# Carrying phases from chunk to chunk: an addition in place instead of a transfer or a matrix product, and three kinds of edges in TensorE's order

## The chip, the core and the metric

One core of one Trainium2 chip. The time is the device time of one launch in microseconds (us). Three runs of the kernel before gave a median of 533.52 us, from 533.45 to 533.83.

## What is computed

A gated linear attention, then a mixture of experts that picks one expert per token. Batch 4, 8 heads, 768 tokens, head size 48; 3072 rows of 384 for the experts, 8 experts with 1024 hidden units, all float32.

```python
mag = np.sqrt(a_re * a_re + a_im * a_im)
scale = np.minimum(mag, 0.999) / (mag + 1e-06)
a_re_n, a_im_n = (a_re * scale, a_im * scale)
for t in range(S):
    ar, ai = (a_re_n[:, :, t, :, None], a_im_n[:, :, t, :, None])
    new_re = ar * S_re - ai * S_im
    new_im = ar * S_im + ai * S_re
    kv = np.einsum('bhd,bhe->bhde', k[:, :, t], v[:, :, t])
    S_re, S_im = (new_re + kv, new_im)
    y[:, :, t] = np.einsum('bhd,bhde->bhe', q[:, :, t], S_re)
# x: y as 3072 rows of 384
e_idx = np.argmax(x @ w_gate, axis=1)
# out = softmax gate * sigmoid gate * relu(x @ w1[e]) @ w2[e], e = e_idx of the row
```

## The kernel before, in words

The complex decay of a step is written as a length and an angle. The lengths of a batch up to a token are then running sums of logarithms, and the angles are running sums too, so a chunk of 128 tokens can be computed at once: q and k are scaled by the running length and turned by the running angle, and what is left are ordinary products of matrices, with a state of 96 x 48 per head that passes from chunk to chunk.

There are 24 chunks of 128 tokens (6 per batch, 4 batches), a token to a partition and the 384 numbers of 8 heads along it. Chunks are prepared in groups of 1, 1, 2, 2, and then 3 chunks. For a group, `prep_exp` makes the logarithms of the lengths and the tangents of the angles on ScalarE and VectorE; `decay` takes the running sum of the logarithms with a matrix product by a triangle (L521, tile `cs`), exponentials of it, and scales q and k; `prep_trig` takes the arctangent; `turns` takes the running sum of the angles (L574, also `cs`), in units of whole turns; `phase` takes the sine and the cosine (tile `trig`). ScalarE holds one set of function tables at a time, so it changes between exponentials and sines with a load (L228).

The sum of the angles goes over a batch, not a chunk, so each chunk needs the last row of the chunk before. After the sum, VectorE rounds it (L578), subtracts the whole turns (L579, in place of the angles, tile `ai`) and takes the size for the cosine (L585). The last row, on partition 127, is the carry. There are two ways for it. Up to the fourth group (`g <= CARRY`), 32 rows of the result are multiplied by a matrix that has ones for the last of them (L576, `sel`), into the same bank as the sum of the next chunk. From the fifth group on, the row is moved to partition 0 by a transfer on SyncE's queue (L584, 18 times), and VectorE adds it to the first row of the next chunk's angles before their sum is taken (L556, 15 times; the first chunk of a batch takes none).

Per chunk, the main order is: turn k (L622, 8 transposes at L94, copy L632), half of the scores (L664, mask L665), turn q, the other half, the gates' rows of the chunk before (`rows_and_gates`, L245; L705 copies the rows to `xn`, which is stored), `state` (L644 brings in the old state, L649 adds the new products, L653 scales it) and `values` (L678 products of the scores with v, L684 of q with the state, both into `xo`; L688 copies it). Sums, phases and the routing are mixed into that order, some chunks ahead.

In the attention stage the order on each engine isn't written by hand. A scheduler takes the instructions as the program gives them, with a rank (`urge` moves some ahead) and its own estimate of when inputs are there. `after(ins, prev, ...)` adds an edge for the order of one engine alone, with no wait on a semaphore. The experts' stage (L1172, L1235) starts near 280 us and is not touched; nor is the recurrence as a fallback, in a branch that these inputs don't take, except that it gets a new copy of its inputs.

## Time and profile before

| | |
|---|---|
| median of 3 runs | 533.52 us (533.45 to 533.83) |
| the profiled execution | 535.06 us, span 533.3 us |
| busy: TensorE, VectorE, ScalarE | 93%, 64%, 59% of the span |
| granted TensorE clock, mean | 0.97 |

The span is the time from the first to the last instruction of the profiled execution. Engines: PE is TensorE (PEld its loads of weights), DVE VectorE, ACT ScalarE, POOL GpSimd, SP SyncE, and SPq is what SyncE issues to the DMA engines. L574 is line 574 of the kernel before. The granted clock is a share of 2.4 GHz.

### The profile page before, as it was taken

The page shows a single profiled execution, that of the slowest core. Times are in us where ns is not written, and L with a number is a line of the kernel's source. Part 1 is how long each engine was busy: PE and PEld are TensorE (multiplying, and loading weights), DVE is VectorE, ACT ScalarE, POOL GpSimd, SP SyncE. Part 2 cuts the span into 40 slices and gives each one's busy share as a digit, 9 for nine tenths or more (in the row PEclk, how much of TensorE's full clock was granted, in tenths as well). Part 3 has the DMA queues.
Part 4 walks back from the last instruction along what each step waited for, and adds up shares of the span by engine and source line. Part 5 has one row for each costly group of instructions (what it writes and reads, how often), then busy time and mean ns, then how long its engine had stood idle before and what let it go on. Part 6 is the DMA issues. An engine that isn't in the chain of part 4 may idle for free.

```text
span 533.3 us, 10970 instructions
## 1 busy us (share of the span) xinstructions
PE 495.2 (93%) x4191; PEld 427.8 (80%) x4191; DVE 340.6 (64%) x801; ACT 314.2 (59%) x581; POOL 116.3 (22%) x134
## 2 busy tenths in 40 slices
PE   2899896999989999999989899999999999999992
PEld 0378574877877878778787789999999999999992
DVE  5579678998877988898857646444353636355220
ACT  7678677887858789657624236355452726354220
POOL 4002002030110203033310544412334232111112
PEclk9799989999989999999999799999999999999998
DMA  8664542526235321104424565537163544431001
GB/s 285 199 216 137 120 132 61 164 67 179 72 75 149 45 77 49 29 31 135 143 56 145 161 170 180 165 82 235 44 205 120 173 149 142 142 115 50 15 27 45
DMA packets 46898, 63.84 MB, mean 120 GB/s; under 512 B 11769, under 2 KB 38668, under 8 KB 46836
## 3 DMA queue, kind: packets, MB, share of 16 engines
q1 hardware_dynamic: 38708, 53.63, 33.6%
q0 software_dynamic: 8128, 9.42, 6.2%
q8 instruction: 35, 0.57, 0.5%
q14 instruction: 27, 0.22, 0.2%
HBM read 53.92 MB, written 9.88 MB: 120 GB/s over the span
## 4 chain that ended last, share of the span: by engine, by line
PE 59%; issue 16%; DVE 8%; DMA 7%; ACT 5%; POOL 3%; POOLq 0%; SPq 0%; DVEq 0%; ACTq 0%
PE acc L1172 12%; PE up L1235 11%; PE tr L94 6%; PE sc L664 5%; PE cs L574 4%; PE xo L678 4%; PE tr L245 4%; PE cs L521 3%; POOL out_dram L1185 3%; PE xo L684 2%; DMA carry<-ai 2%; PE st L649 2%; DMA xd<-xn 1%; DMA ar<-in_a_re_dram 1%; DMA raw<-in_moe_w_dram 1%
## 5 line engine op out<-in xcount | busy, mean ns | idle before, releaser
L1240 DVE SCALAR_TENSOR_TENSOR hl<-up,hh 128x464 fp32r<-128x464 f32 (+7 forms) x64 | 37.7, 589 | 69.8 <-ACT hh L1239 69.5
L1239 ACT ACTIVATE hh<-up 128x464 fp32r<-128x464 f32 (+7 forms) x64 | 33.0, 516 | 72.5 <-PE up L1235 72.5
L1235 PE MATMUL up<-xh,w1h 128*128 128x464 f32 (+7 forms) x192 | 69.1, 360 | 0.2 <-ACT xh L1022 0.2
L1235 PE MATMUL up<-xl,w1h 128*128 128x464 f32 (+7 forms) x192 | 68.1, 355 | 0.0
L1235 PE MATMUL up<-xh,w1l 128*128 128x464 f32 (+7 forms) x192 | 67.8, 353 | 0.0
L1172 PE MATMUL acc<-hh,w2h 128*128 128x464 f32 (+6 forms) x168 | 61.8, 368 | 0.0
L1172 PE MATMUL acc<-hl,w2h 128*128 128x464 f32 (+6 forms) x168 | 59.8, 359 | 1.5 <-DVE hl L1240 1.5
L1172 PE MATMUL acc<-hh,w2l 128*128 128x464 f32 (+6 forms) x168 | 59.8, 356 | 0.0
L1185 POOL DMA_INDIRECT out_dram<-y,sid x28 | 31.7, 1134 | 125.2 <-ACT y L1207 122.2
L664 PE MATMUL sc<-qt,kt 96*128 96x128 f32 x384 | 52.4, 279 | 0.0
L664 PEld LDWEIGHTS sc<-qt,kt 96*128 96x128 f32 x384 | 47.2, 191 | 3.3 <-issue 1.7
L1116 POOL DMA_INDIRECT rows<-xd,sid x28 | 35.5, 1267 | 57.7 <-DVE w1l L211 29.2
L211 DVE TENSOR_TENSOR w1l<-raw,w1h 128x512 fp32r<-128x512 f32 x48 | 30.7, 685 | 18.9 <-ACT w1h L210 18.8
L678 PE MATMUL xo<-scores,v 128*48 128x128 f32 x384 | 42.7, 279 | 0.0
L211 DVE TENSOR_TENSOR w2l<-raw,w2h 128x512 fp32r<-128x512 f32 x48 | 30.6, 688 | 14.6 <-ACT w2h L210 14.3
L1062 POOL DMA_INDIRECT table<-entry,addr x20 | 28.1, 1404 | 53.5 <-DVE addr L1058 49.3
L1235 PEld LDWEIGHTS up<-xl,w1h 128*128 128x128 f32 x192 | 36.3, 189 | 1.6 <-DVE xl L1023 0.4
L210 ACT CAST w1h<-raw 128x512 fp32r<-128x512 f32 x48 | 27.1, 619 | 17.9 <-DMA raw<-in_moe_w_dram 17.9
L1235 PEld LDWEIGHTS up<-xh,w1h 128*128 128x128 f32 x192 | 36.5, 190 | 1.3 <-ACT xh L1022 0.4
L544 POOL COPY rcs<-rcs 24x48 f32<-24x48 f32 (+2 forms) x10 | 5.4, 540 | 146.2 <-DMA rcs<-re 95.6
L1235 PEld LDWEIGHTS up<-xh,w1l 128*128 128x128 f32 x192 | 36.4, 190 | 1.0
L684 PE MATMUL xo<-qt,state 96*48 96x128 f32 x320 | 36.7, 276 | 0.0
(213 smaller groups left out, 1117.9 us busy)
## 6 DMA issues: line engine op xcount, KB each, us to landing
raw<-in_moe_w_dram SPq DMA_DIRECT2D x32, 768.0 KB
ar<-in_a_re_dram SPq DMA_DIRECT2D x24, 192.0 KB
ai<-in_a_im_dram SPq DMA_DIRECT2D x24, 192.0 KB
k<-in_k_dram SPq DMA_DIRECT2D x24, 192.0 KB
q<-in_q_dram SPq DMA_DIRECT2D x24, 192.0 KB
v<-in_v_dram SPq DMA_DIRECT2D x24, 192.0 KB
xd<-xn SPq DMA_DIRECT2D x24, 192.0 KB
rows<-xd,sid POOLq DMA_INDIRECT x28, 4.3
```

Of the source, the lines that this page charges most:

```text
L94: return nc.tensor.transpose(out=out, in_=in_, identity=ident[p0:p0 + n, p0:p0 + n])
L211: nc.vector.tensor_tensor(out=lo[:, s], in0=raw[:, s], in1=hi[:, s].bitcast(F32), op=ALU.subtract)
L664: nc.tensor.matmul(sp[:, j * P:(j + 1) * P], r["kt"][:D2, h, :], r["qt"][:D2, h, :], start=True, stop=True)
L678: nc.tensor.matmul(op[u * DP:u * DP + D, j * P:(j + 1) * P], vt[c][:, h * D:(h + 1) * D], r["s"][:, h, :], start=True, stop=(cc == 0))
L684: nc.tensor.matmul(op[u * DP:u * DP + D, j * P:(j + 1) * P], xs[:D2, h * D:(h + 1) * D], r["qt"][:D2, h, :], start=False, stop=True)
L1062: ins = nc.gpsimd.indirect_dma_start(out=table, out_offset=bass.IndirectOffsetOnAxis(ap=addr[:, c:c + 1], axis=0), in_=entry[:, c, :], in_ ...
L1116: ins = nc.gpsimd.indirect_dma_start(out=rows[e % 2][:n, i, :], out_offset=None, in_=xd[:known], in_offset=bass.IndirectOffsetOnAxis(ap=id ...
L1172: nc.tensor.matmul(accs[kt][:, :cap], w[:, cs], a, start=(ft == 0 and s == 0), stop=(ft == FT - 1 and s == 2))
L1185: ins = nc.gpsimd.indirect_dma_start(out=out, out_offset=bass.IndirectOffsetOnAxis(ap=id_of(e, i, n, loaded), axis=0), in_=y[:n, :], in_of ...
L1235: nc.tensor.matmul(up[:, :cap], w[:, kt, :], x[:, kt, :], start=(m == 0), stop=(m == 3 * KT - 1))
L1239: nc.scalar.activation(out=hh, in_=up[:, :cap], func=AF.Relu)
L1240: nc.vector.scalar_tensor_tensor(out=hl, in0=up[:, :cap], scalar=0.0, in1=hh.bitcast(F32), op0=ALU.max, op1=ALU.subtract)
```

## The change

The inputs a_re and a_im are reordered on the host: in each chunk, the first token comes last. The triangles of the two running sums are changed to match (`tri_ring`: a strict triangle with a full last row), so that the sums come out in the order of the tokens. The row to which the carry belongs is then on partition 127, as the carry is. VectorE adds it in place, on partitions 96 to 127, with a column that is 2 pi on the last partition and 0 on the others; this is done in all groups. The transfers (L584), the matrix products by `sel` (L576) and two variants that weren't in use go. In TensorE's order, three edges are added: a running sum comes behind the last product of `values` that the program has given so far; the first product of a `state` comes behind the last product of the gates' rows; the first product of `values` comes behind the last one of `state`. The fallback recurrence gets its a_re and a_im in order again by four copies in DRAM, inside its branch.

```diff
+    def tri_ring(name, val):
+        t = tri(name, val, strict=True)
+        nc.gpsimd.affine_select(
+            out=t, in_=t, pattern=[[0, P]], compare_op=ALU.is_ge, fill=val, base=P - 2, channel_multiplier=-1)
+        return t
+    tri_l = tri_ring("tri_l", 0.5)
+    tri_t = tri_ring("tri_t", 1.0 / (2.0 * math.pi))
-    tri_r, tri_o, sel (two casts to F32R, a square mask of ones in the last row)
+    last = const.tile([P, 1], F32, name="last")          # 2 pi on partition 127, else 0
...
+            def behind_values(ins):
+                if "values" in st:
+                    after(ins, st["values"], "values first")
...
@@ decay @@
-                    if g >= SPLIT:
-                        ...
-                    else:
-                        nc.tensor.matmul(lp[:, :HD], tri_l, d["l2"][:, c, :], start=True, stop=True)
+                    ins = nc.tensor.matmul(lp[:, :HD], tri_l, d["l2"][:, c, :], start=True, stop=True)
+                    behind_values(ins)
@@ carried, turns @@
-                if not first and not plain:
-                    nc.vector.scalar_tensor_tensor(
-                        out=fr[0:1, :], in0=st["carry"], scalar=2.0 * math.pi, in1=fr[0:1, :], op0=ALU.mult, op1=ALU.add)
+                if (starts[g] + c) % NC:
+                    row = G[g]["ai"][96:128, c, :]
+                    nc.vector.scalar_tensor_tensor(
+                        out=row, in0=st["carry"], scalar=last[96:128], in1=row, op0=ALU.mult, op1=ALU.add)
...
-                    nc.tensor.matmul(tp[:, :HD], tri_t, fr, start=True, stop=first or not plain)
-                if not first and plain:
-                    nc.tensor.matmul(tp[:, :HD], sel[96:128], st["carry"], start=False, stop=True)
+                ins = nc.tensor.matmul(tp[:, :HD], tri_t, fr, start=True, stop=True)
+                behind_values(ins)
...
-                if g <= CARRY:
-                    st["carry"] = fr[96:128, :]
-                else:
-                    st["carry"] = early.tile([1, HD], F32, name="carry")
-                    nc.sync.dma_start(out=st["carry"], in_=fr[127:128, :])
+                st["carry"] = fr[96:128, :]
@@ state @@
+                    after(ins, sets["gates"], "rows first")          # ins: the product by ident, L644
-                        nc.tensor.matmul(
+                        st["state"] = nc.tensor.matmul(
@@ values @@
+                        if h == 0:
+                            after(ins, st["state"] if cc < NC - 1 else sets["gates"], "states first")
...
+                if cc:
+                    st["values"] = ins
@@ recurrence (fallback) @@
+            a_re_of, a_im_of = in_order("a_re_of", a_re), in_order("a_im_of", a_im)
@@ host @@
+        if name in ("a_re", "a_im"):
+            a = _np.ascontiguousarray(_np.roll(a.reshape(a.shape[0], -1, P, *a.shape[2:]), -1, axis=2).reshape(a.shape))
```

## Rows read from the trace of the kernel before

**Rows 1.** The page: TensorE and the other engines' busy time, share of the span and instructions, and the granted clock in 40 slices of 13.3 us, in tenths.
```profile
PE 495.2 (93%) x4191; PEld 427.8 (80%) x4191; DVE 340.6 (64%) x801; ACT 314.2 (59%) x581; POOL 116.3 (22%) x134
PEclk9799989999989999999999799999999999999998
```

**Rows 2.** Busy time by stretch: from and to, length, busy time (instructions) of TensorE, its weight loads, VectorE, ScalarE, GpSimd, then the granted clock, the DMA engines' share and GB/s.
```profile
127.00:159.00 32.00, 30.04 (x335) 24.40 (x332) 26.92 (x63) 23.92 (x41) 4.26 (x4) 0.96 0.37 100
...
189.00:236.00 47.00, 46.99 (x512) 37.24 (x511) 41.25 (x114) 38.61 (x71) 8.35 (x7) 1.00 0.16 44
```

**Rows 3.** Instructions in order of time (start, duration, engine, line, what): the copy of a chunk's rows on ScalarE, once per chunk. Between the first and the second row lie nine chunks, between the second and the third five.
```profile
99.22 0.48 ACT L705 COPY xn<-tr 128x384 f32<-128x384 f32 x1
...
189.35 0.48 ACT L705 COPY xn<-tr 128x384 f32<-128x384 f32 x1 [0.80 <-PE tr L245]
...
235.77 0.48 ACT L705 COPY xn<-tr 128x384 f32<-128x384 f32 x1
```

**Rows 4.** The chain that ended last, in order of time: start, length of the piece, what. Its three pieces of the carry's transfer.
```profile
87.07 3.34 DMA carry<-ai
...
119.57 4.21 DMA carry<-ai
...
150.07 4.87 DMA carry<-ai
```

**Rows 5.** Groups of instructions by line: busy us, mean ns of one, then the engine's idle time just before them and what ended it. A matrix product of float32 is two records.
```profile
L574 PE MATMUL cs<-ai,tri_t 128*128 128x384 f32 x48 | 23.4, 578 | 12.8 <-DVE ai L556 7.2 <-POOL rcs L544 3.0 <-ACT ai L234 2.6
...
L234 ACT ACTIVATE trig<-ai 128x384 f32<-128x384 f32 x24 | 12.6, 524 | 8.7 <-DVE ai L579 8.4
...
L556 DVE SCALAR_TENSOR_TENSOR ai<-carry,ai 1x384 f32<-1x384 f32 x15 | 8.2, 545 | 5.4 <-DMA carry<-ai 5.4
...
L576 PE MATMUL cs<-ai,sel 32*128 32x384 f32 x10 | 6.0, 690 | 0.1
```

**Rows 6.** Instructions in order of time, 149 to 156 us. In brackets: idle time of the engine before, and what ended it.
```profile
149.25 0.54 DVE L579 TENSOR_TENSOR ai<-cs,rnd 128x384 f32<-128x384 f32 x1
...
151.56 0.95 DVE L622 TENSOR_TENSOR qc<-q,trig 128x768 f32<-128x768 f32 x1
...
152.97 0.64 PE L94 MATMUL tr<-ident,qc 128*96 128x128 f32 x4
...
154.97 0.55 DVE L556 SCALAR_TENSOR_TENSOR ai<-carry,ai 1x384 f32<-1x384 f32 x1 [2.45 <-DMA carry<-ai]
...
155.57 0.93 PE L574 MATMUL cs<-ai,tri_t 128*128 128x384 f32 x2 [1.96 <-DVE ai L556]
```

**Rows 7.** Busy time by stretch, columns as in rows 2: behind two of the waits.
```profile
91.00:95.50 4.50, 4.38 (x14) 2.25 (x14) 4.50 (x7) 3.52 (x7) 0.00 (x0) 0.62 0.70 168
...
156.00:160.00 4.00, 4.00 (x26) 3.57 (x26) 3.20 (x8) 1.48 (x3) 0.00 (x0) 0.57 0.18 49
```

**Rows 8.** Instructions in order of time, 123 to 125 us.
```profile
123.81 0.55 DVE L556 SCALAR_TENSOR_TENSOR ai<-carry,ai 1x384 f32<-1x384 f32 x1 [1.67 <-DMA carry<-ai]
...
124.41 0.91 PE L574 MATMUL cs<-ai,tri_t 128*128 128x384 f32 x2 [0.95 <-DVE ai L556]
```

**Rows 9.** Instructions in order of time, 88 to 95 us.
```profile
88.34 1.25 ACT L234 ACTIVATE t<-lnr,b_eps 128x1152 f32<-128x1152 f32 x1 [3.01 <-DVE lnr L481]
...
90.43 0.55 DVE L556 SCALAR_TENSOR_TENSOR ai<-carry,ai 1x384 f32<-1x384 f32 x1 [0.56 <-DMA carry<-ai]
...
90.91 1.34 DVE L490 SCALAR_TENSOR_TENSOR l<-lnr,t 128x1152 f32<-128x1152 f32 x1
91.12 1.28 PE L574 MATMUL cs<-ai,tri_t 128*128 128x384 f32 x2 [4.27 <-DVE ai L556]
91.34 0.60 ACT L234 ACTIVATE trig<-rnd,b_cos 128x384 f32<-128x384 f32 x1
...
92.78 0.94 DVE L622 TENSOR_TENSOR kc<-k,trig 128x768 f32<-128x768 f32 x1
...
93.77 1.60 PE L94 MATMUL tr<-ident,kc 128*96 128x128 f32 x8
```

**Rows 10.** Instructions in order of time, 16 to 20 us: the first two chunks' phases.
```profile
16.72 0.56 DVE L578 TENSOR_SCALAR rnd<-cs 128x384 f32<-128x384 f32 x1 [2.30 <-PE cs L574]
17.38 0.56 DVE L579 TENSOR_TENSOR ai<-cs,rnd 128x384 f32<-128x384 f32 x1
...
18.09 1.61 PE L576 MATMUL cs<-ai,sel 32*128 32x384 f32 x2
...
19.74 0.56 DVE L578 TENSOR_SCALAR rnd<-cs 128x384 f32<-128x384 f32 x1 [1.41 <-PE cs L576]
```

**Rows 11.** The chain that ended last, in order of time: sums inside a run of products with v, the first and the last of five such places.
```profile
106.89 0.84 PE cs L574 x2
107.73 0.79 PE xo L678 x10
...
237.98 0.84 PE cs L574 x2
238.83 0.36 PE xo L684 x4
```

**Rows 12.** Instructions of VectorE in order of time, 84 us.
```profile
84.00 0.54 DVE L556 SCALAR_TENSOR_TENSOR ai<-carry,ai 1x384 f32<-1x384 f32 x1
84.47 0.15 DVE L1058 TENSOR_SCALAR addr<-row 128x2 uint32<-128x2 f32 x1
```

More of the change, by code (lines that the diff above doesn't have):

```diff
@@ L103, in tri @@
         return t
-    tri_l = tri("tri_l", 0.5)
-    tri_r = const.tile([P, P], F32R, name="tri_r")
-    nc.gpsimd.tensor_copy(out=tri_r, in_=tri_l)
-    tri_t = tri("tri_t", 1.0 / (2.0 * math.pi))
+    def tri_ring(name, val):
[5 more added lines that the diff above has]
+    tri_t = tri_ring("tri_t", 1.0 / (2.0 * math.pi))
     mask = tri("mask", 1.0)
-    tri_o = const.tile([P, P], F32R, name="tri_o")
-    nc.gpsimd.tensor_copy(out=tri_o, in_=mask)
     tri_s = tri("tri_s", 1.0, strict=True, dt=BF16)
@@ L114, in tile_gated_attention_moe @@
     nc.gpsimd.memset(ones_b, 1.0)
-    sel = const.tile([P, P], F32, name="sel")
-    nc.gpsimd.memset(sel, 1.0)
+    last = const.tile([P, 1], F32, name="last")
+    nc.gpsimd.memset(last, 2.0 * math.pi)
     nc.gpsimd.affine_select(
-        out=sel, in_=sel, pattern=[[0, P]], compare_op=ALU.is_ge, fill=0.0,
-        base=-(P - 1), channel_multiplier=1,
-    )
+        out=last, in_=last, pattern=[[0, 1]], compare_op=ALU.is_ge, fill=0.0, base=-(P - 1), channel_multiplier=1)
     iota = const.tile([P, CAP], F32, name="iota")
@@ L550, in carried, with turns @@
             def carried(g, c):
-                first = (starts[g] + c) % NC == 0
-                fr = G[g]["ai"][:, c, :]
-                plain = st["carry"] is not None and st["carry"].shape[0] > 1
-                if not first and not plain:
+                if (starts[g] + c) % NC:
+                    row = G[g]["ai"][96:128, c, :]
                     nc.vector.scalar_tensor_tensor(
-                        out=fr[0:1, :], in0=st["carry"], scalar=2.0 * math.pi, in1=fr[0:1, :], op0=ALU.mult, op1=ALU.add)
-                return first, plain
-            def turns(g, c, taken=None):
-                first, plain = taken or carried(g, c)
+                        out=row, in0=st["carry"], scalar=last[96:128], in1=row, op0=ALU.mult, op1=ALU.add)
+            def turns(g, c, taken=False):
+                if not taken:
+                    carried(g, c)
                 fr = G[g]["ai"][:, c, :]
                 tp = pp.tile([P, 512], F32, name="cs")
-                if g >= TSPLIT:
-                    ah = early.tile([P, HD], F32R, name="ah", bufs=AHB)
-                    al = early.tile([P, HD], F32R, name="al", bufs=AHB)
-                    nc.vector.tensor_scalar(out=ah, in0=fr, scalar1=TURN, scalar2=None, op0=ALU.mult)
-                    nc.vector.scalar_tensor_tensor(
-                        out=al, in0=fr, scalar=TURN, in1=ah.bitcast(F32), op0=ALU.mult, op1=ALU.subtract)
-                    nc.tensor.matmul(tp[:, :HD], tri_o, ah, start=True, stop=False)
-                    nc.tensor.matmul(tp[:, :HD], tri_o, al, start=False, stop=True)
-                else:
-                    nc.tensor.matmul(tp[:, :HD], tri_t, fr, start=True, stop=first or not plain)
-                if not first and plain:
-                    nc.tensor.matmul(tp[:, :HD], sel[96:128], st["carry"], start=False, stop=True)
+                ins = nc.tensor.matmul(tp[:, :HD], tri_t, fr, start=True, stop=True)
+                behind_values(ins)
                 rnd = early.tile([P, HD], F32, name="rnd", bufs=4)
@@ L579, in turns @@
                 nc.vector.tensor_tensor(out=fr, in0=tp[:, :HD], in1=rnd, op=ALU.subtract)
-                if g <= CARRY:
-                    st["carry"] = fr[96:128, :]
-                else:
-                    st["carry"] = early.tile([1, HD], F32, name="carry")
-                    nc.sync.dma_start(out=st["carry"], in_=fr[127:128, :])
+                st["carry"] = fr[96:128, :]
                 nc.vector.tensor_scalar(
@@ L591, in turning @@
                 for c in range(sizes[g]):
-                    taken = carried(g, c)
+                    carried(g, c)
                     yield
-                    turns(g, c, taken)
+                    turns(g, c, True)
                     yield
```

17 lines of the change are left out of this document (11 added, 6 removed).

## The prediction, made before the changed kernel was run

> **What bounds the kernel now.** I read the page's engine table and clock line first [rows 1]: TensorE is busy for 93% of the span, and the granted clock falls under 9 tenths in five of the 40 slices, three of them in the first 160 us. The change touches only the attention stage, which ends near 280 us, so next come the busy time in two stretches of it and the pace of its chunks [rows 2, 3]. From 189 to 236 us TensorE has no idle time to speak of, and five chunks pass between the copies at 189.35 and 235.77: 9.28 us each, which I take for TensorE's own pace. From 99.22 to 189.35 nine chunks take 90.13 us, 10.01 each: 0.73 x 9 = 6.6 us above that pace. So there is time to win before 189 us and next to none behind it; what is won upstream is kept, since TensorE's later work stays the same. The chain that ended last says where it lies: three pieces of it are the transfer that brings a chunk's last row of phases to partition 0, 3.34, 4.21 and 4.87 us [rows 4]. The groups by line say what these cost the engines [rows 5]: VectorE stood 5.4 us before the 15 additions of the carry (L556), and TensorE stood 7.2 us before the running sums of the turns (L574) because of them.
>
> **The change, part by part.** *The carry without a transfer.* 18 transfers and 15 additions on one partition go; 20 additions on partitions 96 to 127 come (chunks 1 to 5 of four batches), with the same 384 elements to a partition, so 0.545 us each by L556 [rows 5]. Without the transfer the addition can stand right behind the subtraction (L579) that makes the carry. Place by place:
>
> A, 149 to 157 us [rows 6]. The carry is there at 149.25 + 0.54 = 149.8; the addition starts at 154.97, the sum at 155.57. TensorE ends the transposes of 152.97 at 153.61 and stands for 1.96 us. What is late next: the other four transposes of the same qc, which was made from 151.56 to 152.51. They could go at once, so the whole wait goes. Behind it the clock was granted at 0.57 from 156 to 160 us [rows 7], between the levels of 1.2 and 2.4 GHz, after TensorE had stood: (1 - 0.57) x 4 = 1.7 us of full-clock work lost. Take 1.96 + 1.7 = 3.7 us; at least 0 (something else late), at most the chain's 4.87 [rows 4].
>
> B, 123 to 125 us [rows 8]. VectorE stands 1.67 us, TensorE 0.95. Take 0.95; 0 to 1.67.
>
> C, 86 to 95 us [rows 9]. TensorE stands 4.27 us before the sum at 91.12, and the clock is 0.62 from 91 to 95.5 us [rows 7], another 0.38 x 4.5 = 1.7 us. But here something else is late next: the transposes at 93.77 need kc, made from 92.78 to 93.72, which needs sines and cosines that end at 91.94, and these stand behind an exponential that ends at 89.59 and a load of function tables. Without the addition and the 0.56 us before it VectorE could start L490 at 89.87 instead of 90.91, and kc at 91.94, some 0.85 us earlier. Take 0.85; 0 to 4.27 + 1.7 = 6.0.
>
> The rest of VectorE's 5.4 us, 5.4 - 2.45 - 1.67 - 0.56 = 0.7, made TensorE wait nowhere (1.96 + 0.95 + 4.27 is its 7.2 already): 0, up to 0.7.
>
> *The early chunks*, where the carry was a second matrix product (L576) into the same bank. Five of these go, 6.0 us of records [rows 5], and an addition takes the place of each; but the old product followed a sum that was already done, and the new sum must wait for the addition. The product at 18.09 lets the rounding start at 19.74, 1.65 us [rows 10]. Now an addition of 0.545 comes first, then a sum of the same columns at the same low clock: 0.55 us later. For the other four the sum is shorter at full clock or TensorE has transposes between: some 0. Take +0.5; from -1 (TensorE freed) to 5 x 0.545 = +2.7.
>
> *Queues and set-up.* SyncE loses 18 issues and their waits; loads and row stores that stand behind them leave earlier, but loads run chunks ahead: 0. The carry is now read by VectorE only, so a tile of phases comes free no later. GpSimd's set-up swaps two casts and a square mask for two selections and a column, hidden behind the first loads and logarithms; uncovered, under 1 us. The host's reordering is before the launch, and the loads keep shapes and sizes. The copies in the fallback recurrence are in a branch that isn't taken: 0.
>
> *TensorE's order.* Three kinds of edges without waits of their own: sums behind the last products with v traced so far, a state's first product behind the gates' rows, the products with v behind the state. The work is unchanged. Sums do lie inside runs of products in the trace: 0.84 us at 106.89, with ten records of products after it, and five such places from there to 237.98 [rows 11]. Moving one back brings the copy of its products some 0.84 us forward and its own phase back by about the run's rest, 0.79 us. Take 0; from -2 (half of 5 x 0.84) to the +8.4 of the last rival.
>
> *VectorE's hand-over.* The addition on one partition overlaps its follower: it starts at 84.00 and lasts 0.54, the follower starts at 84.47, 0.07 us before its end [rows 12]. Where the follower needs the result there is a gap instead: 16.72 + 0.56 = 17.28, next start 17.38, 0.10 us [rows 10]. If an addition at partition 96 loses the overlap on both sides, that is 20 x 2 x (0.07 + 0.10) = 6.8 us of VectorE at worst; half is paid anyway where it directly follows its own input, and VectorE, busy 26.92 of 32 and 41.25 of 47 us [rows 2], has room for most. Take +0.5; 0 to +6.8. The Trainium skill, VectorE: DVE Perf Modes, section Two Vector instructions with no wait between them, has this as a rule: an instruction whose inputs or output start in another group of 32 partitions than the last one's begins only when every earlier one has finished. It speaks against this change; no run here shows it yet.
>
> **Sum.** -3.7 - 0.95 - 0.85 + 0.5 + 0 + 0.5 = -4.5 us. The profiled execution took 535.06 us (the span of 533.3 and 1.8 around it), so it would take 530.6; the median of the runs, 533.52, lies 1.54 lower, which gives **529.0 us**.
>
> **Rivals.** *All of it comes back.* If the scheduler, with no transfer to wait for, also moves what is late next in C, TensorE's 7.2 us and both losses of clock (3.4) go: 533.5 - 10.6 + 0.5 = 523.4. For: the stretch before 189 us runs far above the pace. Against: the table loads fix when sines can be made.
>
> *The wait was hidden.* If in A the next thing is late too (ScalarE's copies, the mask of the scores on VectorE), B and C give 1.8 us, and the early chunks and a hand-over of 1.3 us instead of 0.5 take them back: 533.5. For: VectorE is busy for 0.84 to 0.88 of those stretches. The skill's rule above would make this one likelier. Against: in A VectorE itself stood.
>
> *Sums too late: slower.* TensorE takes its queue in order; a sum behind products can't fill the time while these wait for the mask. ScalarE already stands 8.4 us for turned phases [rows 5]. It decides if the sum's phase is the next thing that ScalarE needs. A run is 32 records, 2.5 us at the 0.79 us for ten [rows 11]; a sum that would have gone inside it loses two thirds, 1.7 us; at five places +8.4, less the 4.5 won: 537.4. Against: most sums feed phases that are used a group later.
>
> **How the numbers follow.** Forecast 0.58 (its own range 525.5 to 532), all of it back 0.14, hidden 0.13, slower 0.15. A measurement of this kernel can tell about 0.2%, 1.07 us, from no change: faster 0.58 + 0.14 = 0.72, same 0.13, slower 0.15. The range reaches from 523.0, just past the first rival, to 535.0, past the hidden wait with 1.5 us of the unknown costs; it leaves out the last rival and a little at the bottom.
>
> **What would show it.** Right: the addition within 1 us of its subtraction; under 2 us of TensorE standing before L574's line for it; no fall of the clock near 150 us; nine chunks between the copies that now lie at 99.22 and 189.35 in 85 to 87 us; the pace behind unchanged at 9.3. Wrong: TensorE standing as long at the same places for sines or masks; gaps around the additions on VectorE of several us in all; ScalarE's wait for turned phases grown beyond 8.4 us; or a gain of this size behind 189 us, where I expect none.

## The result, and the profile after

The changed kernel took **538.43 us** (median of 20 runs, 534.99 to 541.52) beside 533.53 (531.10 to 541.29) for the kernel before on the same chip: ratio 1.0078, 95% interval 1.0055 to 1.0102. It is slower by some 0.8%; I had forecast 529.0. Some executions of either kernel run slower than the rest; each ratio here and below leaves these out, and so isn't the quotient of the two medians. A second set of runs gave 537.29 beside 532.85, ratio 1.0073 (1.0047 to 1.0100). The two profiled executions lie closer together than the medians, 536.20 us (span 534.5) against 535.06, so both kernels were profiled once more: before 531.15, changed 536.45. That pair differs by 5.3 us, like the medians, and stages are compared in it unless another is named.

Of the signs that I had named for being right, three came: the addition stands right behind its subtraction, the clock doesn't fall near 150 us, and the pace behind is about what it was. The nine chunks went faster than I had named. The fifth failed: TensorE stands 8.6 us for the addition before the running sums, where I had named under 2. The page of after, answering to [rows 1]: TensorE is busy for less, VectorE for 8.4 us more, and the clock falls to 5, 8 and 7 tenths in the fourth, sixth and eighth slice.
```profile
PE 486.9 (91%) x4181; PEld 427.2 (80%) x4181; DVE 349.0 (65%) x806; ACT 313.9 (59%) x581; POOL 117.4 (22%) x134
PEclk9995989799999999999998899999999999999998
```
Busy time by stretch in the changed kernel, columns as in [rows 2]; the second row is the place of step A.
```profile
127.00:159.00 32.00, 31.02 (x397) 25.14 (x397) 28.84 (x66) 24.94 (x44) 6.01 (x4) 1.00 0.40 112
149.00:157.00 8.00, 8.00 (x115) 6.37 (x115) 7.10 (x14) 4.79 (x9) 5.61 (x4) 1.00 0.44 94
189.00:236.00 47.00, 46.68 (x572) 37.61 (x571) 43.70 (x114) 37.69 (x69) 8.69 (x8) 1.00 0.15 45
```
TensorE has no idle time at A and the full clock. The addition stands right behind its subtraction, as here on VectorE near 155 us (against the 5.2 us from carry to addition in [rows 6]):
```profile
154.72 0.56 DVE L568 TENSOR_TENSOR ai<-cs,rnd 128x384 f32<-128x384 f32 x1
155.31 0.62 DVE L555 SCALAR_TENSOR_TENSOR ai<-ai,last 32x384 f32<-32x384 f32 x1
155.96 0.36 DVE L570 TENSOR_SCALAR rnd<-ai 128x384 int32<-128x384 int32 x1
```
And the pace: the copies of [rows 3] are now these, the nine chunks take 84.14 us (forecast 85 to 87, before 90.13) and the five behind 9.43 each.
```profile
104.35 0.48 ACT L695 COPY xn<-tr 128x384 f32<-128x384 f32 x1
...
188.49 0.48 ACT L695 COPY xn<-tr 128x384 f32<-128x384 f32 x1 [0.33 <-PE tr L245]
...
235.65 0.48 ACT L695 COPY xn<-tr 128x384 f32<-128x384 f32 x1 [0.48 <-PE tr L245]
```
But the first of them lies 5.1 us later than before. What was won behind 100 us had been lost ahead of it. The groups by line, answering to [rows 5]: TensorE stands longer for the addition (8.6 us) than it did for the carry (7.2), and 14.4 us for the logarithms of the decays (tile `l`), where it was 9.4.
```profile
L564 PE MATMUL cs<-ai,tri_t 128*128 128x384 f32 x48 | 22.9, 561 | 11.6 <-DVE ai L555 8.6 <-POOL rcs L545 3.0
L234 ACT ACTIVATE trig<-ai 128x384 f32<-128x384 f32 x24 | 12.6, 525 | 6.7 <-DVE ai L568 6.6
L555 DVE SCALAR_TENSOR_TENSOR ai<-ai,last 32x384 f32<-32x384 f32 x20 | 12.4, 619 | 0.8 <-ACT ai L234 0.2
L521 PE MATMUL cs<-l,tri_l 128*128 128x384 f32 x48 | 23.3, 575 | 14.4 <-DVE l L494 14.4
```
The last of these in the kernel before:
```profile
L521 PE MATMUL cs<-l,tri_l 128*128 128x384 f32 x48 | 23.6, 584 | 9.4 <-DVE l L490 9.4
```
Of the 8.6 us, 5.5 lie at three of the five early additions (2.36, 0.85 and 2.29, ahead of 71 us), 1.8 at the place of step C, 0.6 at that of step B and 0.7 at 184.5 us.

Where, the order of time shows (changed kernel, 18 to 40 us, chunks 1 and 3 of the early phases; [rows 10] answers to its head):
```profile
18.21 0.56 DVE L568 TENSOR_TENSOR ai<-cs,rnd 128x384 f32<-128x384 f32 x1
18.80 0.36 DVE L570 TENSOR_SCALAR rnd<-ai 128x384 int32<-128x384 int32 x1
19.19 0.62 DVE L555 SCALAR_TENSOR_TENSOR ai<-ai,last 32x384 f32<-32x384 f32 x1
19.87 1.65 PE L564 MATMUL cs<-ai,tri_t 128*128 128x384 f32 x2 [2.36 <-DVE ai L555]
21.55 0.56 DVE L567 TENSOR_SCALAR rnd<-cs 128x384 f32<-128x384 f32 x1 [0.73 <-PE cs L564]
...
27.88 0.55 DVE L568 TENSOR_TENSOR ai<-cs,rnd 128x384 f32<-128x384 f32 x1
28.35 0.68 DVE L651 TENSOR_TENSOR scores<-sc,mask 128x512 f32<-128x512 f32 x1
28.95 0.35 DVE L570 TENSOR_SCALAR rnd<-ai 128x384 int32<-128x384 int32 x1
29.33 0.62 DVE L555 SCALAR_TENSOR_TENSOR ai<-ai,last 32x384 f32<-32x384 f32 x1
30.21 0.91 PE L564 MATMUL cs<-ai,tri_t 128*128 128x384 f32 x2
31.16 0.56 DVE L567 TENSOR_SCALAR rnd<-cs 128x384 f32<-128x384 f32 x1 [0.36 <-PE cs L564]
...
34.05 1.28 ACT L228 ACT_TABLE_LOAD   x1
39.28 2.93 PE L521 MATMUL cs<-l,tri_l 128*128 128x384 f32 x4 [4.82 <-DVE l L494]
```
The kernel before in the same place:
```profile
26.57 0.56 DVE L578 TENSOR_SCALAR rnd<-cs 128x384 f32<-128x384 f32 x1 [0.21 <-PE cs L576]
...
30.50 1.28 ACT L228 ACT_TABLE_LOAD   x1
```
Chunk 3's rounding comes 4.6 us later (31.16 against 26.57), ScalarE's load of the exponential table 3.55 later, and with it the decays of group 2 and chunk 2's copy, 78.94 against 75.39.

In this stretch TensorE also stands more and its clock falls. Busy time from 30 to 60 us, columns as in [rows 2], before and changed:
```profile
30.00:60.00 30.00, 28.41 (x421) 22.85 (x420) 25.35 (x56) 23.32 (x40) 3.78 (x3) 1.00 0.49 137
```
```profile
30.00:60.00 30.00, 21.72 (x193) 16.42 (x192) 21.63 (x50) 21.01 (x37) 0.58 (x1) 0.77 0.39 124
```
The clock is 0.50 from 40 to 48 us in the changed kernel, after TensorE was busy for 0.71 of the 4 us from 36.

The stages of all profiles, in us, those of the experiments below too. "Table" is that load, c2 and c4 the copies of chunks 2 and 4, then the time from chunk 4's to chunk 18's copy, from there to the last (chunk 23), and from the last copy to the end of the span.

| kernel | ratio of times to before | table | c2 | c4 | 4 to 18 | 18 to 23 | rest |
|---|---|---|---|---|---|---|---|
| before, 1st / 2nd | 1 | 30.50 / 30.88 | 75.39 / 75.73 | 99.22 / 99.32 | 136.55 / 132.85 | 39.00 / 38.19 | 258.5 / 259.0 |
| changed, 1st / 2nd | 1.0078 / 1.0073 | 34.05 / 34.17 | 78.94 / 78.64 | 104.35 / 103.21 | 131.30 / 131.39 | 38.36 / 38.41 | 260.5 / 261.7 |
| carry_alone | 1.0156 | 33.73 | 78.90 | 105.77 | 128.64 | 48.37 | 255.0 |
| carry_alone_sid | 1.0128 | 32.94 | 78.11 | 104.93 | 128.63 | 44.07 | 259.8 |
| edges_alone | 1.0311 | 35.27 | 83.02 | 109.04 | 137.92 | 47.04 | 252.7 |
| early_sel | 1.0093 | 33.67 | 82.40 | 107.06 | 131.39 | 38.48 | 262.7 |
| early_sel_late_rows, 1st / 2nd | 1.0039 / 0.9997 | 33.73 / 31.24 | 80.24 / 76.15 | 103.52 / 100.22 | 131.38 / 131.51 | 38.64 / 38.46 | 261.6 / 264.1 |
| no_rows | 1.0022 | 34.22 | 79.50 | 103.23 | 128.28 | 38.26 | 262.7 |
| no_values | 1.0065 | 33.93 | 78.83 | 103.65 | 129.51 | 47.45 | 257.0 |
| no_states | 1.0169 | 33.70 | 82.12 | 107.73 | 131.38 | 38.47 | 262.8 |
| early_sel_no_rows, 1st / 2nd | 0.9980 / 0.9983 | 31.60 / 32.90 | 76.50 / 79.39 | 100.55 / 102.64 | 128.40 / 128.26 | 37.93 / 38.87 | 262.3 / 265.2 |
| prompt | 1.0106 | 36.39 | 80.72 | 104.48 | 131.40 | 43.22 | 260.4 |
| prompt_late_rows | 1.0071 | 35.15 | 79.58 | 102.16 | 131.39 | 39.87 | 259.4 |
| warm_before | 1.0144 | 38.33 | 83.23 | 106.95 | 134.35 | 38.83 | 260.9 |
| warm_after | 1.0259 | 41.23 | 86.12 | 110.18 | 131.40 | 40.37 | 266.1 |

The last copy doesn't mark the same work in all of them. The products that place the rows for the experts (`ident,rows` and `row` into `sc` and `st`) lie behind it in most kernels, with 30 to 32 of their records; in carry_alone, edges_alone and no_values only 0, 6 and 6 records do. There the stage from 18 to 23 is longer and the rest shorter for the same work.

### The profile page after: what moved, and what is told of

It reads as the page before. It is cut to its first block, busy times and chain, and to the rows that moved or that the text cites. A ratio compares the mean times of both kernels' runs of the same rounds, so it can differ in the third digit from the quotient of the medians.

```text
span 534.5 us, 10930 instructions
## 1 busy us (share of the span) xinstructions
PE 486.9 (91%) x4181; PEld 427.2 (80%) x4181; DVE 349.0 (65%) x806; ACT 313.9 (59%) x581; POOL 117.4 (22%) x134
## 4 chain that ended last, share of the span: by engine, by line
PE 58%; issue 16%; DVE 10%; ACT 8%; POOL 3%; DMA 3%; POOLq 0%; SPq 0%; DVEq 0%; ACTq 0%
PE up L1225 13%; PE acc L1162 12%; PE tr L94 6%; PE sc L650 4%; PE tr L245 4%; PE xo L664 3%; PE cs L564 3%; POOL out_dram L1175 3%; PE st L635 2%; PE cs L521 2%; PE xo L672 2%; DMA raw<-in_moe_w_dram 2%; PE st L629 1%; ACT t L234 1%; ACT L228 1%
## 5 line engine op out<-in xcount | busy, mean ns | idle before, releaser
L650 PE MATMUL sc<-qt,kt 96*128 96x128 f32 x384 | 51.2, 278 | 0.0
L1052 POOL DMA_INDIRECT table<-entry,addr x20 | 29.6, 1481 | 64.3 <-DVE entry L309 40.5
L211 DVE TENSOR_TENSOR w1l<-raw,w1h 128x512 fp32r<-128x512 f32 x48 | 30.7, 685 | 18.0 <-ACT w1h L210 18.0
L211 DVE TENSOR_TENSOR w2l<-raw,w2h 128x512 fp32r<-128x512 f32 x48 | 30.8, 686 | 13.3 <-ACT w2h L210 13.1
L664 PE MATMUL xo<-scores,v 128*48 128x128 f32 x384 | 37.1, 278 | 0.0
L521 PE MATMUL cs<-l,tri_l 128*128 128x384 f32 x48 | 23.3, 575 | 14.4 <-DVE l L494 14.4
```

The source lines that it names most:

```text
L211: nc.vector.tensor_tensor(out=lo[:, s], in0=raw[:, s], in1=hi[:, s].bitcast(F32), op=ALU.subtract)
L521: ins = nc.tensor.matmul(lp[:, :HD], tri_l, d["l2"][:, c, :], start=True, stop=True)
L650: nc.tensor.matmul(sp[:, j * P:(j + 1) * P], r["kt"][:D2, h, :], r["qt"][:D2, h, :], start=True, stop=True)
L664: ins = nc.tensor.matmul(op[u * DP:u * DP + D, j * P:(j + 1) * P], vt[c][:, h * D:(h + 1) * D], r["s"][:, h, :], start=True, stop=(cc == 0))
L1052: ins = nc.gpsimd.indirect_dma_start(out=table, out_offset=bass.IndirectOffsetOnAxis(ap=addr[:, c:c + 1], axis=0), in_=entry[:, c, :], in_ ...
```

## The experiments

**A second look at both kernels.** Unchanged code.

> The kernel before once more, for a second profile of it. Theory J (where TensorE's clock falls and returns differs from execution to execution): the transposes of chunk 0 at 21 to 25 us come back to full speed (1.08 us for eight products) up to 4 us later than in the first profile (24.0), chunk 1's copy lands between 51 and 56 us, and the time lies anywhere in 531 to 540. Rival F (executions are alike, the differences are the kernel's): chunk 1's copy at 51.9 within 0.5 us.

> The changed kernel once more, for a second profile and for times beside the others of this call. By its 20 runs its median is 538.4 and the first profile (536.2) lies 2 us under it: theory J expects the difference in stretches at half clock ahead of 130 us or behind 280 us, the order and the number of instructions being the same; chunk 1's copy at 58 to 64 us. Rival F: chunk 1's copy at 61.4 within 0.5 us.

Before came at 531.15 us with chunk 1's copy at 52.28: the early stage is alike in both looks, as rival F said. From chunk 4 to 18 its two executions differ by 3.7 us: 3.0 at step A and 0.64 at step B, where TensorE stood 0.31 us and not 0.95. In the second look the carry's transfer was issued at 149.54 and TensorE stood 0.54 us, not 1.96, with the full clock behind it:
```profile
149.54 1.42 SPq L584 DMA_DIRECT2D carry<-ai  x1
...
153.01 0.55 DVE L556 SCALAR_TENSOR_TENSOR ai<-carry,ai 1x384 f32<-1x384 f32 x1 [1.03 <-DMA carry<-ai]
...
153.61 0.91 PE L574 MATMUL cs<-ai,tri_t 128*128 128x384 f32 x2 [0.54 <-DVE ai L556]
```
So 3 of the 3.7 us that I had put on A were an accident of one execution (chunk 9 to chunk 10 took 12.68 us there and 10.02 here, chunk 10 to 11 10.69 and 10.33). The changed kernel's second look agrees with its first within 1.2 us at each copy; chunk 1's lies at 60.54, a little outside rival F's half microsecond.

**The two halves of the change.** carry_alone: the three `after(...)` calls of the diff left out. edges_alone: the three added to the kernel before, nothing else.

> The changed kernel without its three rules for TensorE's order (values first, rows first, states first): ring layout and addition in place alone. Theory E (two early losses): the addition in front of the sums of chunks 1 to 3 makes ScalarE's table load start near 34 us (before 30.5, changed 34.05), but chunk 1's state products and products with v stand ahead of decay group 2 again, so chunk 1's copy lands at 55 to 56 us (before 51.89, changed 61.42); by the end about 3 us under the changed kernel, 533 to 536. Rival O (TensorE's order alone costs the time): early copies as before (52 to 53), 528 to 531. Rival C (the early loss does not reach the end, what is behind 189 us sets it): early copies as by theory E, time within 1 us of the changed kernel's 538.4.

> The kernel before with the three rules for TensorE's order, and its carry (selection product early, a transfer later) as it was. Theory E: table load at 30.5 us as before, but TensorE waits near 32 to 40 us for decay group 2 with chunk 1's state and values queued behind the gates of chunk 0, and its clock falls: chunk 1's copy at 56 to 58 us (before 51.89); the stalls of the carry's transfer at 123 to 157 us remain; 535 to 539. Rival O (the order alone costs the time): 538 or more. Rival A (the addition in place alone costs it): as before, 533.5, chunk 1's copy at 52. Rival C (early loss never reaches the end): chunk 1's copy late, time within 1 us of before's 533.5.

541.14 us beside 532.86 (1.0156, 1.0114 to 1.0199) and 549.22 (1.0311, 1.0251 to 1.0371): each half alone is slower than both together, so the loss doesn't divide between them. Theory E had the early copies nearly right (54.35; 59.92 where TensorE's clock came back only near 33 us) and missed the times; rival O had edges_alone's time and missed carry_alone's by 10 us. The end of the attention was not in either theory (18 to 23: 48.37 and 47.04 us, in part for work that lies behind the last copy elsewhere; from chunk 18's copy to the end of the span it is 303.4 us in carry_alone, 300.1 in the changed kernel's second look). For carry_alone the trace shows what it waits for: VectorE stands 3.88 us for a list that GpSimd writes and a transfer reads back, with the scores queued behind it.
```profile
255.13 2.77 POOL L1048 DMA_INDIRECT table<-entry,addr  x1 [0.30 <-DVE state L637]
...
262.53 0.33 SPq L1069 DMA_DIRECT2D slots<-table  x1
264.01 0.17 DVE L1081 TENSOR_SCALAR sid<-slots 116x4 uint32<-116x4 f32 x1 [3.88 <-DMA slots<-table]
264.09 0.68 DVE L649 TENSOR_TENSOR scores<-sc,mask 128x512 f32<-128x512 f32 x1
```

**That stand, moved.** carry_alone_sid is carry_alone and one more rule for VectorE:
```diff
-                        slot_ids(0, 1)
+                        after(slot_ids(0, 1), st["scored"], "scores first")
```


> The kernel with ring and addition in place alone (541.1), and one more rule: VectorE's conversion of the slot numbers, which waits for a list read back by a transfer, stands behind the scores of the chunk at hand instead of ahead of them. Theory D (that kernel was slow by VectorE standing 3.88 us for the list with the scores queued behind it, and by what TensorE's clock then lost): no stand of VectorE over 1 us between 255 and 270 us, the last copy at 274 to 277 (282.78), the time 533 to 537. Rival C (the carry in place itself makes it slow): 540 to 542.

540.42 us (1.0128), 0.7 us under carry_alone and in the range of rival C. The last copy came 5.2 us earlier (277.63), nearly as theory D said, but the rest is 4.8 us longer, with the products that place the rows behind the copy again. VectorE still stood 4.07 us for the list, now ahead of the next chunks' choice of experts. Half of theory D fell: the place of the reader isn't the cause, the list itself is late. One of its last three writes by GpSimd takes 2.77 us in carry_alone and 3.36 in this kernel, where all three take 0.97 in the changed kernel.

**The early carry.** early_sel puts the selection product back for groups 0 to 3 (chunks 1 to 5; the expectations speak of 1 to 3); late_rows lets the rows-first rule begin at chunk 4:
```diff
-                if (starts[g] + c) % NC:
+                if (starts[g] + c) % NC and g > CARRY:
...
+                if early_carry:
+                    nc.tensor.matmul(tp[:, :HD], sel[96:128], st["carry"], start=False, stop=True)
...
-                    after(ins, sets["gates"], "rows first")
+                    if i >= 4:
+                        after(ins, sets["gates"], "rows first")
```


> The changed kernel, but the carry of chunks 1 to 3 (groups 0 to 3) enters by a selection product as before, and in place only from group 4 on; the three rules for TensorE's order stay. Theory E: the table load is back at 30.5 us (changed 34.05), chunk 1's copy at 57 to 58 us (before 51.89, changed 61.42); 534 to 536. Rival O: chunk 1's copy no earlier than 60, time within 1 us of the changed kernel's 538.4. Rival C (early loss does not reach the end): chunk 1's copy at 57 to 58 and yet 537.5 to 539.5.

> The changed kernel, but with the selection product for the carries of chunks 1 to 3, and the rule that puts a chunk's state behind the rows and gates of an earlier chunk only from chunk 4 on, so that TensorE's first 33 us of work stand in the order of before. Theory E: table load at 30.5 us, chunk 1's copy at 52 us, and the gains between 52 and 159 us (9 us in the changed kernel's profile) stay in part: 527 to 531. Rival C (what is behind 189 us, or the experts' part, sets the end): chunk 1's copy at 52, the copies behind 189 us where they were, 537 to 539. Rival G (the middle's gain was only the early loss caught up): the copy near 159 us where it was, 532 to 534.

> The kernel with the early selection products and late rows-first rule once more, for a second profile. In its first profile eight transposes still took 1.94 us at 25.71, and the table load came at 33.73. If TensorE's clock is back by 25 us here as in both profiles of before: the table load at 30.5 to 31 us, chunk 2's copy at 75.5 to 77 (first profile 80.24), the end of the attention at 269 to 271, a profiled time of 528 to 532. If it comes back at 28 us or later again: as in the first profile, 534 to 537, and theory P then can't tell this kernel's early order from the clock.

539.83 us (1.0093) for early_sel, and 536.87 (1.0039, 1.0000 to 1.0077), then 532.41 (0.9997, 0.9966 to 1.0027) for early_sel_late_rows. In the first profile of each the table load was at most 0.5 us earlier than in the changed kernel, and theory E looked wrong. The second profile of early_sel_late_rows shows what lay over it: TensorE's clock. Its eight transposes of qc, in the first and then in the second execution, with the table load behind each:
```profile
25.71 1.94 PE L94 MATMUL tr<-ident,qc 128*96 128x128 f32 x8
...
33.73 1.28 ACT L232 ACT_TABLE_LOAD   x1
```
```profile
24.72 1.08 PE L94 MATMUL tr<-ident,qc 128*96 128x128 f32 x8
...
31.24 1.28 ACT L232 ACT_TABLE_LOAD   x1
```
With the clock back as early as in both looks at before, the load is at 31.24 (before 30.50 and 30.88, changed 34.05 and 34.17) and chunk 2's copy at 76.15. The whole attention then ends at 270.19, before's second look at 270.36. So the early carry in place costs some 3 us at the load. The times of early_sel don't show it (1.0093, the changed kernel 1.0073), and its only profile has the clock late; the last experiment shows it without the rows-first rule.

**Does a delay ahead of 50 us reach the end?** 13 idle products in TensorE's order ahead of the first sum of turns, in both kernels:
```diff
+                            for t in range(13):
+                                wp = pp.tile([P, 512], F32, name="st", bufs=1)
+                                st["warm"] = nc.tensor.matmul(wp[:, :P], ident, ident, start=True, stop=True)
```


> The kernel before with 13 idle products (identity by identity, into the bank of the state, read by nobody) in TensorE's order between the second decay sum and the first sum of turns, where it stood for 3 us; the order of all else is the same. Theory J: the first sums of turns (2.25 us for two at half clock) and the transposes of chunk 0 run at full clock or reach it some us earlier, chunk 1's copy 2 to 4 us earlier, and the time 529 to 533. Rival D (the early stage waits for ScalarE and the transfers, not for TensorE's clock): chunk 1's copy within 1 us of before's 51.9, time 533 to 535.

> The changed kernel with the same 13 idle products in the same place. Theory E (the loss is the longer chain of phases and the rows-first order, the low clock follows from TensorE standing): the stand of 2.4 us ahead of chunk 1's sum and that of 4.8 us ahead of decay group 2 remain, the clock falls again near 38 us, chunk 1's copy at 59 to 62; time 536 to 539. Theory J alone (the clock's start decides): chunk 1's copy at 55 to 57, time 532 to 535, no more than 2 us above the kernel before with the idle products.

They were meant to fill 3 us and took 10.88, so the sums came 7.3 us late, and TensorE, busy since 9.3 us, still ran at half clock until 31 (by its durations):
```profile
12.38 10.88 PE L529 MATMUL st<-ident 128*128 128x128 f32 x26
23.05 2.77 PE L578 MATMUL cs<-ai,tri_t 128*128 128x384 f32 x4
```
As a test of the clock both failed. As a delay they serve: chunk 2's copy comes 7.5 us later than in the second look at the same kernel without the products, in both, the last copies 9.8 and 8.9, and the times are 542.69 us beside 532.85 and 547.37 beside the changed kernel's 537.29, 9.8 and 10.1 more. Nothing behind absorbs the delay; rival C falls, and the stage ahead of chunk 2 is on the path. (The times grow by more than the 7.5 us; in warm_after VectorE stands 3.3 us for the list too.)

**Ranking the early additions first.** prompt wraps the early addition and its sum in the scheduler's high priority; prompt_late_rows adds the late rows-first rule.
```diff
+                    if g <= CARRY:
+                        s.enter_context(tc.high_priority(offset=1000))
```


> The changed kernel with the early carries (chunks 1 to 3) ranked first by the scheduler: the addition stands ahead of the absolute value and of a product kc or qc on VectorE, and the sum ahead of transposes and scores on TensorE. Theory P (the longer chain of the early phases is what the end pays for): the table load at 32 to 32.8 us (changed 34.05 and 34.17; before 30.50 and 30.88) where TensorE's clock is back by 25 us, chunk 2's copy at 77 to 77.7 (changed 78.94 and 78.64), the time 1 to 2 us under the changed kernel's 537 to 538.5. Rival B (the order of everything behind is what costs): the table load as by theory P, the time within 0.7 us of the changed kernel's.

> The kernel of the run with prompt early carries, and the rows-first rule only from chunk 4 on. Theory S (chunk 2 waits for its phases and decays, not for chunk 1, so chunk 1's lateness has slack): chunk 1's copy at 54 to 56 us (changed 61.42 and 60.54), chunk 2's copy where the run with prompt early carries has it, and the time within 1 us of that run. Rival R (chunk 1's lateness is on the path): 3 us or more under that run.

538.07 us (1.0106) and 537.73 (1.0071): a miss. The addition now stood ahead of the absolute value, but the products kc behind it came later (transposes at 22.89 and 22.24, in the changed kernel at 21.31), the clock came back at 28 and 27 us, and the table load went to 36.39 and 35.15; theory P's size is not confirmed by this pair. The second kernel had chunk 1's copy 7.5 us earlier than the first (55.42, 62.94). Their medians differ by 0.3 us and their ratios by 0.35%, inside both intervals, but VectorE stood 4.6 us for the list in the first and 0.2 in the second, so the pair doesn't settle theory S. The next run does: without the rows-first rule alone, chunk 1's copy is at 54.95 (60.54 in the changed kernel's second look) and chunk 4's at 103.23 (103.21). Chunk 1's lateness has slack.

**The three rules one by one.** Each left out of the changed kernel alone.

> The changed kernel without the rows-first rule alone; carry in place, values first and states first stay. Theory S: chunk 1's copy at 54 to 55 us as in the run with the carry alone (54.35; changed 61.42), chunk 2's copy at 78.5 to 79 as in the changed kernel; what differs at the end then comes from the order behind 80 us. If the rule helps behind, 538 to 542; rival R (the rule's early cost is on the path): 533 to 535.

> The changed kernel without the values-first rule alone. Its order on VectorE puts the conversion of the slot numbers ahead of the last scores but two, as in the kernel with the carry alone. Theory D: VectorE stands 3 to 4 us for the list near 262 us, last copy at 278 to 284 us, time 540 to 544. Rival V (the rule's own place in the attention's middle decides): the copies at 99 to 250 us differ from the changed kernel's by over 2 us, with no stand for the list.

> The changed kernel without the states-first rule alone. The conversion of the slot numbers stands behind the scores as in the changed kernel. Theory D: no stand for the list, the early copies as in the changed kernel (chunk 1's 60 to 62 us, chunk 2's 78.5 to 79), the time within 1.5 us of the changed kernel's 537.3 to 538.4. Rival W (this rule carries the price or the gain behind 80 us): a difference of over 2 us that is seen in the copies between 99 and 235 us.

534.38 us (1.0022, 0.9992 to 1.0052), 538.58 (1.0065) and 542.75 (1.0169, 1.0112 to 1.0225). The **rows-first rule** costs some 3 us, though not by either theory: chunk 4's copy stays (103.23, 103.21), and the gain lies behind it, 128.28 us from chunk 4 to 18 against 131.39. Every profile with the carry in place and this rule has 131.3 to 131.5 there, but for no_values with 129.5; every one without it 128.3 to 128.6. TensorE's busy time from 100 to 240 us, in the changed kernel and without the rule:
```profile
100.00:240.00 140.00, 136.28 (x1655) 109.86 (x1647) 128.48 (x315) 111.78 (x198) 24.73 (x20) 1.00 0.32 86
```
```profile
100.00:240.00 140.00, 139.75 (x1687) 114.21 (x1679) 130.82 (x320) 115.80 (x205) 24.20 (x21) 1.00 0.34 91
```
It stands 3.7 us with the rule and 0.25 without, in small waits (us in total, times, longest; changed kernel, then without the rule):
```profile
PE cs L564 <- DVE ai L555: 1.3, 2, 0.7
PE tr L245 <- ACT qt L617: 1.2, 5, 0.3
PE tr L94 <- DVE qc L607: 1.0, 2, 0.6
```
```profile
PE tr L245 <- ACT qt L617: 0.2, 1, 0.2
```
The gates' products wait for ScalarE to empty a bank (1.2 of the 3.5 us in these rows), and the rule keeps the state's products, which could go meanwhile, behind them; that the other two waits come from the same rule is shown by their absence without it, how is not. In the early stage the rule makes TensorE stand too, and that costs nothing at chunk 4: from 30 to 60 us it is busy for 25.63 us without the rule and 21.72 with it.
```profile
30.00:60.00 30.00, 25.63 (x302) 20.62 (x301) 23.95 (x57) 22.34 (x42) 3.45 (x3) 0.94 0.46 144
```
Leaving out **states first** costs some 5 us, 4.5 of it ahead of chunk 4 (107.73). Leaving out **values first** gains 1.9 us from chunk 4 to 18 and loses 9 behind it, by VectorE standing 4.0 us for the list as theory D said; yet the time, 538.58, is 1.4 us under its range, the part behind the last copy being 4.7 us shorter, with most of the products that place the rows ahead of it.

**Both costs out.** early_sel_no_rows: the selection product for the early carries, and no rows-first rule.

> The changed kernel with selection products for the carries of chunks 1 to 3 and without the rows-first rule; carry in place from group 4 on, values first and states first stay. Theory N (the early loss and the rule's cost are two separate prices, and the carry in place gains in the middle: without the rule chunk 4 to chunk 18 took 128.3 us against 132.9 in the second profile of before): where TensorE's clock is back by 25 us, chunk 2's copy at 75.5 to 77 us, chunk 18's at 228 to 229.5 (second profile of before 232.17), the time 528.5 to 531.5. Rival M (the middle only caught up an early loss, without the loss there is nothing to gain): chunk 18's copy at 231 to 233, the time 532 to 534, as before.

> The kernel with early selection products and without the rows-first rule once more (first time 531.2 beside 532.5 of before, ratio 0.998 from 0.994 to 1.002), for a second set of times and a second profile. Theory N: the ratio again under 1.000, chunk 18's copy at 228 to 230 us where TensorE's clock is back by 25 us, 3 to 4 us later where it is not. Rival M: ratio 1.000 or above, chunk 18's copy at 231 or later with the clock back early.

531.24 us beside 532.54 (0.9980, 0.9944 to 1.0016) and 532.91 beside 532.78 (0.9983, 0.9953 to 1.0014). In the first profile chunk 18's copy is at 228.95 and the last at 266.88, 3.2 and 3.5 us ahead of before's second look: theory N for the attention.
```profile
228.95 0.48 ACT L701 COPY xn<-tr 128x384 f32<-128x384 f32 x1 [0.49 <-PE tr L249]
...
266.88 0.48 ACT L701 COPY xn<-tr 128x384 f32<-128x384 f32 x1 [0.62 <-DVE q L699]
```
In the second profile the clock came back late again and c4 lies 2.1 us later; from chunk 4 to 18 it is 128.26. But the part behind the last copy is 3.3 and 6.2 us longer than before's, and both intervals hold 1: a gain over the kernel before isn't shown. Beside the changed kernel's 1.0073 these ratios are lower by 0.9%, some 4.9 us: with the two costs out, the whole loss is gone. no_rows (1.0022) differs from this kernel by the early carry alone: 0.4%, some 2 us, is that carry's price in time.

## Why the prediction was wrong

- **The early chunks** are the step that failed first: forecast +0.5 us, at most +2.7; measured +3.3 to +3.55 at the table load, and +3.9 at chunk 4 (103.21 against 99.32). I priced the addition at one chunk and let transposes hide the others. But from rounding to rounding (chunks 0 to 3) the three steps went from 3.02, 4.34 and 2.49 us to 4.00, 4.99 and 4.62. Before, the large sum was done early and only the short selection product waited for the carry; now addition and sum both do, and the addition takes its turn on VectorE behind the absolute value and, for chunk 3, behind a mask of the scores (27.88 to 29.33). I had named under 2 us of TensorE standing for the addition; at these early places alone it is 5.5. The selection product put back brings the load to 31.24 and 31.60 us and chunk 4 to 100.22 and 100.55, where the clock came back early.
- **TensorE's order**, forecast 0, is the second: the rows-first rule costs 3 us from chunk 4 to 18. I weighed the sums' place only (their rule left out gave 1.9 us in that stretch and lost more behind it); the rule that keeps the state's products back I did not weigh at all. My slower rival had the right sign and near the right time (537.4), but its mechanism isn't what happened: ScalarE's wait for phases fell from 8.4 to 6.6 us.
- **A** was the right mechanism, mis-sized: 3.7 us in the execution I read, about 0.5 in the next. I also subtracted the 1.54 us by which that execution lay over the median; the accident was counted in both. **B** was 0.95 us there, 0.31 in the next and 0.6 in the changed kernel. At **C** TensorE's stand fell from 4.27 and 4.07 us to 1.80 in both looks at the changed kernel, but the clock still falls behind it, to 0.50 and 0.70 from 97 to 102 us.
- **The gain of the middle** is there in every profile: from chunk 4 to 18 without the rows-first rule the carry in place takes 128.3 to 128.6 us, alone or with the other rules, against 132.85 (134.35 in warm_before): some 4.3 us, close to the 4.65 of A and B, but not made of them, since in the execution with 132.85 TensorE stood under 1 us for the carry between 100 and 240 us. How it comes about is not settled. (In carry_alone TensorE has done about 1 us more of its products by chunk 4's copy, so the gain there is nearer 3.)
- **The pace of 9.28 us** that I took for TensorE's own was not its floor: the same five chunks (13 to 18) take 44.8 to 44.9 us without the rows-first rule and with the carry in place, 8.97 each, and 47.2 in the changed kernel. So there was something to win, and to lose, behind 189 us too.
- **VectorE's hand-over** lies inside the bound: the addition lasts 0.619 us, not 0.545, and its neighbours start 0.03 us behind each other's end (155.28, 155.31; 155.93, 155.96) where the old addition overlapped by 0.07 [rows 12]. VectorE is busy for 8.4 us more; five more additions (2.7 us) and the bound of 6.8 make 9.5. The Trainium skill, VectorE: DVE Perf Modes, section Two Vector instructions with no wait between them, calls an instruction held that starts only when every earlier one has finished; the trace agrees. No run isolates what it costs in time.
- **The sum as measured**, second looks: +3.9 to chunk 4, -1.5 to chunk 18 (-4.6 with the carry as in no_rows, +3.1 by the rule), +0.2 to the last copy, +2.7 behind: +5.3 us of span.
- The last 2.7 are open in part. In the 40 us behind the last copy the granted clock is 0.96 in before's second look, and 0.87 in the changed kernel's second and in early_sel_no_rows' first; busy time is nearly the same:
```profile
270.00:310.00 40.00, 36.00 (x193) 30.84 (x193) 24.69 (x83) 13.22 (x30) 12.21 (x8) 0.96 0.51 138
```
```profile
273.00:313.00 40.00, 36.07 (x179) 30.45 (x178) 23.89 (x82) 12.92 (x29) 11.36 (x8) 0.87 0.50 132
```
```profile
267.00:307.00 40.00, 35.69 (x177) 30.54 (x176) 23.77 (x81) 12.80 (x29) 11.48 (x8) 0.87 0.44 130
```
  (0.96 - 0.87) x 40 = 3.6 us of full-clock work would cover it, and over all profiles with the same work behind the last copy the rest is longer where the clock is lower: 259.0 and 259.4 us at 0.96, 258.5 to 260.9 at 0.91, 261.6 to 265.2 at 0.87, 266.1 at 0.79. But the first looks at before and at the changed kernel both have 0.91 there and still differ by 2.0 us (258.5, 260.5), so the clock isn't shown to be the whole of it. Why it falls for longer, with the experts' code unchanged, no run tells.

## What to carry to other kernels

A dependency that is added costs what it does to the chain it is in, followed instruction by instruction through each engine's queue, and the early chain, with nothing behind it to fill the time, is where to look first. A stall that one profiled execution shows is worth what a second execution shows too, and never both that stall and the execution's distance to the median. A rule that only orders work can take away fillers, as the rows-first rule did here; look for the short waits that the work it holds back now covers.

## What was not expected of the hardware

- Where TensorE's clock comes back differs between executions of kernels whose early products are the same: it was back at 23 to 25 us in both looks at before and at the changed kernel, at 28 to 29 in early_sel and in one of the two profiles each of early_sel_late_rows and early_sel_no_rows, and near 33 in edges_alone. Between the two profiles of early_sel_late_rows it goes with copies 3 to 4 us later, of early_sel_no_rows 2 to 3. In warm_before TensorE had been busy from 9.3 us on and came back no sooner than 31.
- In most traces the view shows a granted clock of 1.00 in those stretches, although eight transposes take 1.94 us instead of 1.08 (the changed kernel, 1.92 us at 21.31). In five, both looks at before among them, it shows the low clock (0.60 from 20 to 24 us in before); there the first sum still starts with a record of 0.56 to 0.72 us, where it is 0.98 in the others (but for warm_before and warm_after, whose idle products come first). So a clock that is low from the start on seems not to be recorded, and the durations are what tells.
- An indirect write of GpSimd (`table<-entry`) takes from 0.97 to 4.0 us; the changed kernel has both, 0.97 at 255.7 and 3.58 at 89.1. In the long ones of carry_alone and carry_alone_sid VectorE was splitting weights (L211) at the time, but so it was in two of 0.97 in the changed kernel, and at 89.1 it was at the logarithms. What makes them long is not shown.
